# Where the first kernel of an S4 layer is loaded, and who adds the skip weights

## The chip, the cores and the metric

One core of a Trainium2 chip. The metric is the device time of one execution in microseconds, the median of several runs. A profile is one more execution, recorded instruction by instruction. Engines are named as in the profile: PE (matrix products; PEld its weight loads), DVE (vector), ACT (scalar functions), POOL (GpSimd) and SP (which here only issues DMAs).

## What is computed

Four layers in a row on x of 2048 positions by 640 channels, each with a layer norm and a residual: a long convolution with an S4 kernel, attention with one shared key and value head, the same convolution again, the same attention again.

```python
dt = jnp.exp(log_dt)[:, None]
P = jnp.exp((dt * A)[:, :, None] * l[None, None, :])
K = jnp.einsum("dn,dnl,dn->dl", Cc, P, dt * Bc).real     # kernel, 640 x 2048
...
y = irfft(rfft(pad(u)) * rfft(pad(K)))[..., :L] + u * Dskip
```

The convolution is done with Fourier transforms. Adding `u * Dskip` is the same as adding Dskip to the kernel's value at position 0, and this is how the program does it, before it transforms the kernels.

## The kernel before

The program has three parts that matter here.

The kernel generator, `_kgen`, makes K in 20 units on PE, ACT and DVE. Each finished unit is copied by ACT into a staging tile `kst`, and after units 7, 15 and 19 SP stores it into `kd` in device memory: five kernels of 128 channels each, 128 partitions by 16 positions by 128 channels. Position 0 is partition 0, the first 128 values. Kernels 0 and 1 are stored after the first 8 units, 2 and 3 after the next 8, kernel 4 at the very end, in four stores of short pieces (L436). During the generator POOL writes the constant first columns of the tables `c` and `s` (L362, L363), two memsets a unit. Near its end POOL issues the eight loads of the transform's weights `wf` (L527).

`kernel_spectra` loads the five kernels back, four into one tile `kts` and the fifth into `ktl`, adds the skip weights (`skip`, a one-row addition on DVE, L656), and transforms each: `raw` multiplies with `wf` on PE in four quarters (L545), ACT copies each quarter out of PSUM (L547), DVE does the butterflies `radix` (L555) and `fft8` (L96, L99) with two scratch tiles, `B` (16 KB a partition) and `R` (8 KB), and SP stores the spectrum into `kh`. The transform of kernel c + 1 on PE overlaps the butterflies of kernel c on DVE.

`conv_layer` then transforms x, multiplies, and transforms back, with the same `B` and `R`.

PE, ACT and DVE run in the order in which the code is written (`manual_schedule`). POOL and SP are queues of their own: a DMA that must wait for something holds everything behind it. The tiles of the convolution (`B`, `R`, `kts` under the tag "wi", `ktl` under "xn") lie in memory that the generator's tiles used before, so the first use of each waits until the generator's last use of that place is over. Such waits are found when the program is built: `B` lies on `kst`, `R` on the generator's rounding and fraction tiles, `kts` and `ktl` on its tables.

Of the kernel before, what the change touches and what calls it, by code (L numbers as in the profile page):

```python
# [11 lines left out]
F32 = mybir.dt.float32  # L12
# [4 lines left out]
ALU = mybir.AluOpType  # L17
# [4 lines left out]
P = 128  # L22
# [3 lines left out]
DC = 128  # L26
NCH = D // DC
# [57 lines left out]

def fft8(nc, A, B, R, sg):

    ADD, SUB = ALU.add, ALU.subtract
    plus, minus = (ADD, SUB) if sg < 0 else (SUB, ADD)
    calls = []

    def tt(*a):
        calls.append(lambda: nc.vector.tensor_tensor(*a))  # L96

    def stt(*a):
        calls.append(lambda: nc.vector.scalar_tensor_tensor(*a, op0=ALU.mult, op1=ADD))  # L99

    tt(B[:, 0:4], A[:, 0:4], A[:, 4:8], ADD)
    tt(B[:, 4:8], A[:, 0:4], A[:, 4:8], SUB)
    tt(R[:, 0:2], A[:, 10:15:4], A[:, 11:16:4], ADD)
    if sg < 0:
        tt(R[:, 2:4], A[:, 11:16:4], A[:, 10:15:4], SUB)
        tt(B[:, 12:16:3], R[:, 0:3:2], R[:, 3:0:-2], ADD)
        tt(B[:, 14:12:-1], R[:, 0:3:2], R[:, 3:0:-2], SUB)
    else:
        tt(R[:, 2:4], A[:, 10:15:4], A[:, 11:16:4], SUB)
        tt(B[:, 12:16:3], R[:, 2::-2], R[:, 1:4:2], SUB)  # L110
        tt(B[:, 14:12:-1], R[:, 2::-2], R[:, 1:4:2], ADD)
    tt(B[:, 8:12:3], A[:, 8:10], A[:, 13:11:-1], plus)
    tt(B[:, 10:8:-1], A[:, 8:10], A[:, 13:11:-1], minus)
    tt(A[:, 0:2], B[:, 0:2], B[:, 2:4], ADD)
    tt(A[:, 8:10], B[:, 0:2], B[:, 2:4], SUB)
    tt(A[:, 4:14:9], B[:, 4:6], B[:, 7:5:-1], plus)
    tt(A[:, 12:4:-7], B[:, 4:6], B[:, 7:5:-1], minus)
    sp, sm = (RT_HALF, -RT_HALF) if sg < 0 else (-RT_HALF, RT_HALF)
    f0, f2, f1, f3s = B[:, 8:10], B[:, 10:12], B[:, 12:14], B[:, 15:13:-1]
    stt(A[:, 2:4], f1, RT_HALF, f0)  # L120
    stt(A[:, 10:12], f1, -RT_HALF, f0)
    stt(A[:, 6:16:9], f3s, sp, f2)
    stt(A[:, 14:6:-7], f3s, sm, f2)
    return calls


def weave(calls, between):

    for i in range(len(calls) + 1):
        for n, call in between:  # L130
            if n == i or (i == len(calls) and n > i):
                call()
        if i < len(calls):
            calls[i]()


class Net:
# [153 lines left out]
    def _kgen(self, ctx):  # L291
        tc, nc, ins = self.tc, self.nc, self.ins
# [126 lines left out]
        def store(u):  # L419
            q, r, _, _, run = units[u]  # L420
            if r == 0 and q > 0:
                KST[q] = bp.tile([P, 32, run], F32, tag="kst", bufs=1, name=f"kst{q}")
            kst = KST[q]
            nc.scalar.activation(kst[:, :, 16 * r : 16 * r + 16],
                                 PK[u].rearrange("p (d j) -> p j d", d=16), AF.Copy)
            if 16 * (r + 1) == run:
                for par in range(2):
                    for jh in range(2):
                        src = kst[64 * par : 64 * par + 64, 16 * jh : 16 * jh + 16, :]
                        if run == 128:  # L430
                            dst = self.kd[2 * q + par, 64 * jh : 64 * jh + 64]
                            nc.sync.dma_start(dst, src.rearrange("p t d -> p (t d)"))
                        else:
                            dst = self.kd[4, 64 * jh : 64 * jh + 64].rearrange(
                                "p (t d) -> p t d", d=DC)[:, :, 64 * par : 64 * par + 64]
                            nc.sync.dma_start(dst, src)  # L436

# [3 lines left out]
        with tc.manual_schedule(engines=engines):  # L443
            for h in range(2):
                phase(0, h)
            for u in range(n + 3):
                now, nxt, prod, tot = u < n, u + 1 < n, 0 < u <= n, 2 <= u < n + 2
                odd = u % 2 == 1
                if u >= 3:
                    store(u - 3)  # L450
# [54 lines left out]
    def conv_setup(self, ctx):  # L505
        tc = self.tc
        if not self.wfs:
            self.conv_weights(self.nc.sync)
        self.cvp = ctx.enter_context(tc.tile_pool(name="cvp", bufs=1, reuse_waits="tile"))

        self.B = self.cvp.tile([P, 16, 256], F32, name="B")
        self.R = self.cvp.tile([P, 8, 256], F32, name="R")

    def conv_weights(self, eng, after=None):

# [121 lines left out]
    def load_spectrum(self, c):  # L637
        A = self.cvp.tile([P, 16, 256], F32, tag="kh", bufs=2, name=f"kh{c}")
        self.nc.sync.dma_start(A.rearrange("p s d -> p (s d)"), self.kh[c])
        return A  # L640

    def kernel_spectra(self):

        nc, cv = self.nc, self.cvp

        kts = cv.tile([P, 4, 16, DC], F32, tag="wi", name="kts")
        ktl = cv.tile([P, 24, DC], F32, tag="xn", name="ktl")
        ks = [kts[:, c] for c in range(4)] + [ktl[:, 0:16]]
        dsk = ktl[0:1, 16:21]
        nc.gpsimd.dma_start(dsk.rearrange("p c d -> p (c d)"), self.ins["A_Dskip"][None, :])  # L650
        for c in range(NCH):
            nc.gpsimd.dma_start(ks[c].rearrange("p t d -> p (t d)"), self.kd[c])

        def skip(c):
            k = ks[c][0:1, 0]
            nc.vector.tensor_tensor(k, k, dsk[:, c], ALU.add)  # L656

        skip(0)
        Z = {0: self.raw(ks[0], "k0")}
        for c in range(NCH):  # L660
            if c + 1 < NCH:
                skip(c + 1)
                Z[c + 1] = self.raw(ks[c + 1], f"k{c + 1}")
            A = cv.tile([P, 16, 256], F32, tag="kh", bufs=2, name=f"kn{c}")
            weave(self.radix(Z.pop(c), A) + fft8(nc, A, self.B, self.R, -1), ())
            nc.sync.dma_start(self.kh[c], A.rearrange("p s d -> p (s d)"))

    def conv_layer(self, nm, first):
# [1 line left out]


        tc, nc, cv = self.tc, self.nc, self.cvp
        B, R = self.B, self.R
        tt = nc.vector.tensor_tensor
        with tc.manual_schedule(engines={mybir.EngineType.PE, mybir.EngineType.Activation,
                                         mybir.EngineType.DVE}):
# [5 lines left out]
            self.norm_next(nm)  # L682
            if first:
                self.kernel_spectra()

            def X(c, tau):
                return self.x[:, tau, c * DC : (c + 1) * DC]
# [549 lines left out]
```

## Time and profile before

| | us |
|---|---|
| median of 3 runs | 3103.51 |
| lowest and highest run | 3099.85, 3104.56 |
| the profiled execution | 3100.43 |
| its span, first to last instruction | 3098.6 |
| PE busy in the span | 2850.6 (92%) |
| ACT busy | 2387.1 (77%) |
| DVE busy | 1436.4 (46%) |
| POOL busy | 41.8 (1%) |

Times in a timeline are counted from the start of the span. The generator runs until about 338, the kernels' spectra until about 437, the first convolution until 664; the first attention layer, the second convolution and the second attention layer follow. A row of the timeline gives start, length, engine, line, operation and tiles; in brackets stands how long the engine had been idle before and what it then waited for. Arrows read from the result: `zk<-kts,wf` is zk made from kts and wf.

### The profile page before, as it was taken

To read this page: it belongs to the slowest core of one execution; us is meant where nothing else is said; L and a number is where in the kernel's file an instruction comes from. 1 tells how busy PE (TensorE), PEld (TensorE's weight loads), DVE (VectorE), ACT (ScalarE), POOL (GpSimd) and SP (SyncE) were. 2 spreads that over 40 slices of the span, in tenths; PEclk is the share of its full clock that TensorE was granted. 3 is DMA by queue.
4 is the path that set the end of the run, shared out by engine and by line. 5 is a ranking of instruction groups with operands and counts; after the bars stand their busy time and mean duration, and the time that the engine had idled before them with its cause. 6 is when DMAs were issued, how large, how long until landed. Compare 5 with 4: busy or idle time off the path is not lost. (4 is left out here: it accounts for less than half of the span.)

```text
span 3098.6 us, 52133 instructions
## 1 busy us (share of the span) xinstructions
PE 2850.6 (92%) x21636; PEld 1349.7 (44%) x21636; DVE 1436.4 (46%) x1855; ACT 2387.1 (77%) x2769; POOL 41.8 (1%) x114
## 2 busy tenths in 40 slices
PE   2888998949899999999999899498999999999999
PEld 0555887847322333333333489464223333233333
DVE  7888799973122232232332399932222222222223
ACT  5777343224799999999999623055999999999997
POOL 0000000000100000000000000000000000000000
PEclk9999999979999999999999999799999999999999
DMA  6011451114310010100100210132010100100100
GB/s 142 18 29 24 168 218 55 33 30 131 116 27 25 21 26 23 25 25 21 27 25 22 111 55 28 26 111 89 22 27 23 40 25 21 44 25 21 44 18 22
DMA packets 73630, 153.45 MB, mean 50 GB/s; under 512 B 22836, under 2 KB 28980, under 8 KB 69764
## 3 DMA queue, kind: packets, MB, share of 16 engines
q1 hardware_dynamic: 67336, 132.36, 14.6%
q0 software_dynamic: 4080, 16.67, 1.4%
q8 instruction: 174, 2.85, 0.4%
q10 hardware_dynamic: 1968, 0.98, 0.1%
q14 instruction: 72, 0.59, 0.1%
HBM read 93.42 MB, written 44.50 MB: 45 GB/s over the span
## 5 line engine op out<-in xcount | busy, mean ns | idle before, releaser
L1038 ACT ACTIVATE pt<-scd 128x1024 f32<-128x1024 f32 x1024 | 942.2, 1116 | 7.5 <-PE scd L1034 5.8
L1038 ACT ACTIVATE pt<-scb 128x1024 f32<-128x1024 f32 x1024 | 942.2, 1116 | 7.0 <-PE scb L1034 5.4
L1048 PE MATMUL pod<-pt,vt 128*32 128x512 f32 x4096 | 547.1, 606 | 4.4 <-DVE on L1065 0.3
L1048 PE MATMUL pob<-pt,vt 128*32 128x512 f32 x4096 | 546.8, 606 | 4.4 <-DVE on L1065 0.5
L1034 PE MATMUL scd<-qpd,kt 62*128 62x512 f32 x2048 | 386.0, 451 | 6.0 <-PEq L983 5.6
L1034 PE MATMUL scb<-qpb,kt 62*128 62x512 f32 x2048 | 386.0, 451 | 5.8 <-PEq L983 5.5
L1034 PEld LDWEIGHTS scd<-qpd,kt 62*128 62x128 f32 x2048 | 166.0, 185 | 402.0 <-ACT pt L1038 392.6
L1034 PEld LDWEIGHTS scb<-qpb,kt 62*128 62x128 f32 x2048 | 166.0, 185 | 401.6 <-ACT pt L1038 392.4
L1096 DVE TENSOR_TENSOR x<-pyd,x 128x320 f32<-128x320 f32 x146 | 71.7, 491 | 561.1 <-PE pyd L1108 561.1
L1096 DVE TENSOR_TENSOR x<-pyb,x 128x320 f32<-128x320 f32 x146 | 71.7, 491 | 547.8 <-PE pyb L1108 547.8
L1068 DVE RECIPROCAL rc<-rc 128x512 f32<-128x512 f32 x62 | 207.9, 3353 | 2.1
L1048 PEld LDWEIGHTS pod<-pt,vt 128*32 128x32 f32 x4096 | 80.6, 108 | 178.2 <-issue 160.2
L1048 PEld LDWEIGHTS pob<-pt,vt 128*32 128x32 f32 x4096 | 80.6, 108 | 178.2 <-issue 160.2
L416 PE MATMUL pk<-s,m 128*64 128x32 f32 x1280 | 130.8, 295 | 13.3 <-DVE s L407 13.3
L416 PE MATMUL pk<-c,e1r 128*64 128x32 f32 x1280 | 132.1, 297 | 11.4 <-DVE c L406 11.2
L416 PEld LDWEIGHTS pk<-c,e1r 128*64 128x64 f32 x1280 | 105.3, 221 | 79.6 <-issue 52.1
L727 PE MATMUL ya<-Aa,wi 128*128 128x128 f32 x640 | 78.0, 285 | 50.5 <-DVE Aa L96 47.2
L727 PE MATMUL yc<-Ac,wi 128*128 128x128 f32 x640 | 78.4, 286 | 46.8 <-DVE Ac L96 43.7
L574 PE MATMUL za<-xna,wf 128*128 128x256 f32 x512 | 113.1, 383 | 2.3 <-ACT xna L690 2.3
L416 PEld LDWEIGHTS pk<-s,m 128*64 128x64 f32 x1280 | 108.1, 226 | 15.9 <-DVE s L407 15.9
L574 PE MATMUL zc<-xnc,wf 128*128 128x256 f32 x512 | 111.5, 379 | 2.7 <-ACT xnc L690 2.7
L576 ACT ACTIVATE Aa<-za 128x1024 f32<-128x1024 f32 x16 | 16.4, 1024 | 118.4 <-PE za L574 117.4
(276 smaller groups left out, 3170.6 us busy)
## 6 DMA issues: line engine op xcount, KB each, us to landing
kh<-kh SPq DMA_DIRECT2D x10, 2048.0 KB
kh<-kn SPq DMA_DIRECT2D x5, 2048.0 KB
qhd<-qh SPq DMA_DIRECT2D x40, 256.0 KB
qld<-ql SPq DMA_DIRECT2D x40, 256.0 KB
qpb<-qhd SPq DMA_DIRECT2D x256, 40.0 KB
qpd<-qhd SPq DMA_DIRECT2D x256, 40.0 KB
ot<-on SPq DMA_DIRECT2D x216, 40.0 KB
wf<-in_c_wf POOLq DMA_DIRECT2D x16, 512.0 KB, 7.8
```

The lines of the kernel that those rows point to most:

```text
L416: nc.tensor.matmul(PK[u][64 * par : 64 * par + 64, 32 * d : 32 * d + 32], e[u][:, d, par], c[u][:, d, par], start=first, stop=not first)
L574: nc.tensor.matmul(zv[:, :, c, kk], self.wf[:, t + 4 * h, j, c, kk], x, start=(n == 0), stop=(n == 3))
L576: nc.scalar.activation(A.rearrange("p (o s) d -> p o s d", o=2)[:, :, 2 * t : 2 * t + 2], z.rearrange("p (c o e) -> p o c e", c=2, o=2), A ...
L727: nc.tensor.matmul(y[:, s * DC : (s + 1) * DC], self.wi[:, t, j, c_, kk], v[:, 2 * t + c_, kk], start=(i == 0), stop=(i == 3))
L1034: nc.tensor.matmul(sc[:, 512 * par : 512 * par + 512], kt[rows, 128 * t : 128 * t + 128], qps[nb, hg, pr][rows], start=True, stop=True)
L1038: nc.scalar.activation(pt, sc, AF.Exp, scale=SCALE)
L1048: nc.tensor.matmul(po[32 * j : 32 * j + 32], vt[:, t], pts[step, j // 2][:, 512 * (j % 2) : 512 * (j % 2) + 512], start=(t == 0), stop=(t ...
L1068: nc.vector.reciprocal(rc, rc)
L1096: nc.vector.tensor_tensor(xh, py, xh, ALU.add)
```

## The change

Kernel 0 is no longer loaded into `kts` but into R's place: the scratch tile is now taken in two turns under one tag, first as the target of kernel 0's load, then, once PE has read it, as the butterflies' scratch. `kts` holds kernels 1 to 3, `ktl` kernel 4. The load of the skip weights into `ktl` and the five DVE additions are gone. Instead POOL issues five accumulating DMAs: for kernels 0 to 3 in the generator, right after their stores, onto the stored rows in `kd`; for kernel 4 after its load, onto the row in `ktl`. In the second convolution the scratch tile is taken in `conv_layer` rather than in `conv_setup`.

```diff
@@ store
+                for c in range(2 * q, min(2 * q + 2, NCH - 1)):
+                    self.skip(c, self.kd[c, 0:1, 0:DC])
@@ conv_setup
-        self.R = self.cvp.tile([P, 8, 256], F32, name="R")
+
+    def scratch(self, nm):
+        return self.cvp.tile([P, 8, 256], F32, tag="R", bufs=1, name=f"R{nm}")
@@ kernel_spectra
+    def skip(self, c, k):
+
+        self.nc.gpsimd.dma_start(k, self.ins["A_Dskip"][None, c * DC : (c + 1) * DC], accum_op=ALU.add)
+
+        ks = [self.scratch("k0").rearrange("p a b -> p (a b)").rearrange("p (t d) -> p t d", t=16)]
         kts = cv.tile([P, 4, 16, DC], F32, tag="wi", name="kts")
         ktl = cv.tile([P, 24, DC], F32, tag="xn", name="ktl")
-        ks = [kts[:, c] for c in range(4)] + [ktl[:, 0:16]]
-        dsk = ktl[0:1, 16:21]
-        nc.gpsimd.dma_start(dsk.rearrange("p c d -> p (c d)"), self.ins["A_Dskip"][None, :])
+        ks += [kts[:, c] for c in range(3)] + [ktl[:, 0:16]]
         for c in range(NCH):
             nc.gpsimd.dma_start(ks[c].rearrange("p t d -> p (t d)"), self.kd[c])
-
-        def skip(c):
-            k = ks[c][0:1, 0]
-            nc.vector.tensor_tensor(k, k, dsk[:, c], ALU.add)
-
-        skip(0)
+        self.skip(NCH - 1, ks[4][0:1, 0])
         Z = {0: self.raw(ks[0], "k0")}
         for c in range(NCH):
             if c + 1 < NCH:
-                skip(c + 1)
                 Z[c + 1] = self.raw(ks[c + 1], f"k{c + 1}")
             A = cv.tile([P, 16, 256], F32, tag="kh", bufs=2, name=f"kn{c}")
+            if c == 0:
+                self.R = self.scratch("k")
...
@@ conv_layer
             if first:
                 self.kernel_spectra()
+            else:
+                self.R = self.scratch(nm)
+            R = self.R
```

PE, ACT and DVE keep their order; what moves is POOL's queue and a few waits. First POOL, from the end of the generator to the kernels' loads, before. What an instruction waits for stands in brackets: an engine by its name, DMAs issued by SP as DMAHW with a lane's number, those issued by POOL as DMASW.

```order
L363 MEMSET s_19_2437 128x32 [waits DVE_49,Pool_49]
L527 DMA wf<-in_c_wf 128x1024 [waits DMAHW4_49,DMAHW3_49,DMAHW5_49,DMAHW2_49,DMAHW6_49,DMAHW1_49,DMAHW7_49,DMAHW0_49,PE_49]
L527 DMA wf<-in_c_wf 128x1024 x7
L650 DMA ktl<-in_A_Dskip 1x16x40 [waits DMASW0_49,DVE_49,PE_49]
L652 DMA kts<-kd 128x2048 [waits DMAHW6_49,DMAHW7_49,DMASW1_49,Pool_49]
L652 DMA kts<-kd 128x2048 [waits DMAHW1_49,DMAHW0_49,DMASW2_49]
L652 DMA kts<-kd 128x2048 [waits DMAHW3_49,DMAHW2_49,DMASW3_49]
L652 DMA kts<-kd 128x2048 [waits DMAHW5_49,DMAHW4_49,DMASW4_49]
L652 DMA ktl<-kd 128x2048 [waits DMAHW6_49,DMAHW1_49,DMAHW7_49,DMAHW0_49,DMASW5_49]
```

The same place in the changed kernel, where Rk is kernel 0's place in the scratch tile:

```order
L363 MEMSET s_19_2441 128x32 [waits DVE_49,Pool_49]
L648 DMA kd<-in_A_Dskip 16x8 [waits DMAHW4_49]
L531 DMA wf<-in_c_wf 128x1024 [waits DMAHW5_49,DMAHW3_49,DMAHW7_49,DMAHW1_49,PE_49]
L531 DMA wf<-in_c_wf 128x1024 x3
L531 DMA wf<-in_c_wf 128x1024 [waits DMASW0_49]
L531 DMA wf<-in_c_wf 128x1024 [waits DMASW1_49]
L531 DMA wf<-in_c_wf 128x1024 [waits DMASW2_49]
L531 DMA wf<-in_c_wf 128x1024 [waits DMASW3_49]
L659 DMA Rk_2718<-kd 128x2048 [waits DMASW4_49,DMAHW7_49,DVE_49,Activation_49]
L659 DMA kts<-kd 128x2048 [waits DMASW5_49,DVE_49,DMAHW1_49,Activation_49,Pool_49]
L659 DMA kts<-kd 128x2048 [waits DMAHW3_49,DMASW6_49]
L659 DMA kts<-kd 128x2048 [waits DMAHW5_49,DMASW7_49]
```

Before, every load of a kernel stood behind a DMA that waits for PE, the load of the skip weights into ktl. Now a wait for PE comes only with ktl's own load, the next row. The last four wf loads wait for the four accumulating transfers, whose lanes they use again (the third transfer stands one row ahead of the memset, the first two around the memset of unit 11).

Then DVE, from the end of kernel 0's `radix` into `fft8`, before:

```order
L555 TENSOR_TENSOR kn_2871<-Azk_2724 128x512 [waits Activation_49]
L555 TENSOR_TENSOR kn_2871<-Azk_2724 128x512
L96 TENSOR_TENSOR B<-kn_2871 128x1024 [waits DMAHW4_49,DMAHW3_49,DMAHW5_49,DMAHW2_49,DMAHW6_49,DMAHW1_49,DMAHW7_49,DMAHW0_49,DVE_49]
L96 TENSOR_TENSOR B<-kn_2871 128x1024
L96 TENSOR_TENSOR R<-kn_2871 128x512 [waits DVE_49]
```

And now:

```order
L559 TENSOR_TENSOR kn_2873<-Azk_2727 128x512 [waits Activation_49]
L559 TENSOR_TENSOR kn_2873<-Azk_2727 128x512
L96 TENSOR_TENSOR B<-kn_2873 128x1024 [waits DMAHW4_49,DMAHW3_49,DMAHW5_49,DMAHW2_49,DMAHW6_49,DMAHW1_49,DMAHW7_49,DMAHW0_49,DVE_49]
L96 TENSOR_TENSOR B<-kn_2873 128x1024
L96 TENSOR_TENSOR Rk<-kn_2873 128x512 [waits DMASW4_49,DVE_49,PE_49]
```

The first write of B waits for the stores of kernel 4 out of `kst` in both; the first write of R now also waits for kernel 0's load and for PE's last read of it. Elsewhere on DVE only the five additions are missing.

More of the change, by code (lines that the diff above doesn't have):

```diff
@@ L672, in conv_layer @@
         tc, nc, cv = self.tc, self.nc, self.cvp
-        B, R = self.B, self.R
+        B = self.B
         tt = nc.vector.tensor_tensor
```

## The prediction

> **What bounds the kernel now.** The page first, ACT's busy tenths in 40 slices:
>
> ```profile
> ACT  5777343224799999999999623055999999999997
> ```
>
> The nines are the two attention layers, most of the span, where ACT has hardly a pause. The change touches none of that; it touches the few microseconds where the kernel generator ends and the kernels' spectra begin, in the fifth slice. I cut that stretch out with the table by windows (columns: stretch, length, PE, PE weight load, DVE, ACT, POOL busy, granted clock, share of the DMA engines, GB/s).
>
> ```profile
> 338.59:344.68 6.09, 0.00 (x0) 0.00 (x0) 2.52 (x13) 2.09 (x3) 2.62 (x5) 1.00 0.66 226
> 351.60:374.40 22.80, 22.80 (x207) 22.80 (x205) 15.98 (x25) 6.15 (x6) 0.53 (x1) 1.00 0.33 92
> 374.40:437.40 63.00, 58.92 (x522) 58.26 (x520) 62.86 (x99) 24.53 (x37) 0.00 (x0) 1.00 0.61 234
> 437.40:664.50 227.10, 176.52 (x1040) 160.66 (x1041) 225.96 (x247) 56.23 (x116) 0.31 (x1) 0.89 0.16 55
> ```
>
> First PE stands still for 6.1 us; then PE is the busy engine until the first kernel is transformed; from 374 to 664 DVE never rests (62.86 of 63.00 us, 225.96 of 227.10). The list of waits says the same: DVE's only waits between 343 and 664 are these two, and PE's one wait for a load is the gap.
>
> ```profile
> DVE kn L555 <- ACT Azk L547: 10.8, 4, 4.0
> DVE kts L656 <- DMA kts<-kd: 4.8, 2, 2.5
> PE zk L545 <- DMA kts<-kd: 6.1, 1, 6.1
> ```
>
> So the end of this layer is set by one chain: load of kernel 0, PE's raw transform in four quarters, ACT's four copies, then DVE, which runs without a wait for some 300 us. Whatever brings the fourth copy forward brings all of DVE's work forward, and after 664 attention starts on what DVE left. The timeline shows that chain's head, and POOL's queue, which issues the loads:
>
> ```profile
> 302.74 0.16 POOL L362 MEMSET c<- 128x32 f32 x1 [6.79 <-DVE e1r L399]
> 309.92 0.16 POOL L363 MEMSET s<- 128x32 f32 x1 [7.02 <-DVE m L404]
> 319.53 4.37 POOL L527 DMA_DIRECT2D wf<-in_c_wf  x8 [9.45 <-PE pe L380]
> 338.24 0.30 PE L416 MATMUL pk<-s,m 128*64 128x32 f32 x2
> 338.63 0.51 POOL L650 DMA_DIRECT2D ktl<-in_A_Dskip  x1 [14.73 <-PE pk L416]
> 339.22 2.12 POOL L652 DMA_DIRECT2D kts<-kd  x4
> 344.68 0.58 PE L545 MATMUL zk<-kts,wf 128*128 128x128 f32 x1 [6.14 <-DMA kts<-kd]
> 350.54 1.02 ACT L547 ACTIVATE Azk<-zk 128x1024 f32<-128x1024 f32 x1 [9.83 <-PE zk L545]
> 354.05 1.02 ACT L547 ACTIVATE Azk<-zk 128x1024 f32<-128x1024 f32 x1 [2.49 <-PE zk L545]
> 357.63 1.02 ACT L547 ACTIVATE Azk<-zk 128x1024 f32<-128x1024 f32 x1 [2.55 <-PE zk L545]
> 361.20 1.02 ACT L547 ACTIVATE Azk<-zk 128x1024 f32<-128x1024 f32 x1 [2.55 <-PE zk L545]
> 363.47 2.35 DVE L96 TENSOR_TENSOR B<-kn 128x1024 f32<-128x1024 f32 x2
> 660.45 2.04 PE L727 MATMUL ya<-Aa,wi 128*128 128x128 f32 x8 [36.44 <-DVE Aa L96]
> ```
>
> The kernels' loads stand in POOL's queue behind the load of the skip weights into ktl, and that one waits 14.73 us for PE's last pk product. All four kts loads are held by a wait that only ktl's place in memory needs.
>
> **The change, part by part.** *The PE gap.* Kernel 0 now goes to R's place, and no load in front of it waits for PE: of the engines, its waits now name DVE and ACT alone. It can be issued right behind the wf loads (319.53 + 4.37 = 323.9) at the earliest, and at the latest when the generator's last products on DVE end:
>
> ```profile
> 330.44 1.21 DVE L407 TENSOR_TENSOR s<-s,m 128x1024 f32<-128x1024 f32 x1
> 330.00:332.00 2.00, 1.18 (x20) 0.94 (x19) 2.00 (x4) 0.60 (x1) 0.00 (x0) 1.00 0.93 361
> 332.00:334.00 2.00, 2.00 (x44) 2.00 (x41) 1.93 (x8) 0.00 (x0) 0.00 (x0) 1.00 0.06 23
> 342.00:344.00 2.00, 0.00 (x0) 0.00 (x0) 0.24 (x3) 0.00 (x0) 0.00 (x0) 1.00 1.00 411
> DMA to landing us min/median/max: 5.4/9.4/13.2
> ```
>
> That is 331.65. Both ends give the same landing, since the wf loads fill the DMA engines until 332. From there 1.05 MB at 411 GB/s take 2.55 us, so the data is across at 334.6; the shortest landing of a kts load, 5.4 us counted from 332, gives 337.4. Both lie ahead of 338.54, where PE's last pk product ends. The 6.14 us gap goes entirely. The wf loads were issued from POOL in 4.37 / 8 = 0.55 us each beside DVE's products, so I count no hold-up of POOL by DVE. [...]
>
> *The slow first quarter.* The first copy starts 5.86 us after PE's first matmul, the second 3.51 us later and the fourth 3.57 us after the third. In the group's row the slowest matmul takes just over twice the median:
>
> ```profile
> L545 PE MATMUL zk<-kts,wf x512: 275/275/582, 344.7 to 403.8; 128*128 128x128 f32 x171
> 347.00:348.00 1.00, 1.00 (x6) 1.00 (x6) 1.00 1.00 414
> 350.00:351.00 1.00, 1.00 (x11) 1.00 (x11) 1.00 1.05 431
> ```
>
> (The last two rows are slices of one microsecond for this line: PE, weight load, clock, DMA share, GB/s.) Six matmuls in one slice, eleven in the other, with the DMA engines equally full: so it is not the loads that slow PE, but the standstill before. Without a standstill the first quarter takes 3.57 us: 2.29 us less. The granted clock in these rows stays at 1.00 and does not show it. [...]
>
> *The skip additions on DVE.* Five one-row additions leave DVE. Two lie ahead of the chain, in DVE's wait. Three lie in the unbroken part:
>
> ```profile
> 374.29 0.27 DVE L656 TENSOR_TENSOR kts<-kts,ktl 1x128 f32<-1x128 f32 x1
> 374.49 0.67 DVE L555 TENSOR_TENSOR kn<-Azk 128x512 f32<-128x512 f32 x1
> 390.12 0.27 DVE L656 TENSOR_TENSOR kts<-kts,ktl 1x128 f32<-1x128 f32 x1
> 405.95 0.27 DVE L656 TENSOR_TENSOR ktl<-ktl 1x128 f32<-1x128 f32 x1
> ```
>
> Each shifts the next start by 0.20 us (374.29 to 374.49), three by 0.60. PE's pace of 4 x 3.57 = 14.3 us a kernel stays ahead of DVE's 15.6 (390.12 - 374.29 - 0.20), so DVE stays the bound.
>
> *The skip transfers on POOL.* Five accumulating transfers are added. The trace of before has no such transfer; the nearest row is the plain load of the skip weights, 1.7 us from issue to landing, and the farthest of the neighbourhood is 13.2 us. The third and fourth stand around the memset at 309.92 and wait for stores of the second pair of kernels:
>
> ```profile
> 312.00:315.00 3.00, 2.25 (x24) 1.15 (x22) 3.00 (x4) 1.70 (x3) 0.00 (x0) 1.00 0.00 0
> 328.17 1.22 DVE L404 TENSOR_TENSOR m<-m,s 128x1024 f32<-128x1024 f32 x1
> DMA to landing us min/median/max: 1.7/3.4/5.2
> ```
>
> (In the last row the first figure is the skip weights' load, the last one kernel 4's.) The stores' traffic is over by 312 (the first row has none); with a microsecond for the receipt, an estimate, the fourth transfer is issued by 313. Behind it on POOL stand the wf loads, which cannot go before 319.53 anyway: 6 us of cover. The memset behind the third is first read at 328.17: 18 us of cover. At 1.7 us the transfers have landed by 315, at 13.2 us by 326; that would hold the last wf load for some 3 us, while the ones before it keep the DMA engines full until past 330. I take 1.7, the nearest row, and a cost of nothing; the far end costs nothing either. The fifth runs in SBUF after ktl's load and is needed only by kernel 4, some 50 us later. A gain from them is excluded, as nothing waits for their results earlier than for the old additions.
>
> *A new neighbour for DVE's first B.* B lies where the last stores into kd read, and DVE's first write of B waits for those stores, before as after. Now it was due at 363.47 and found them done:
>
> ```profile
> 357.61 0.53 POOL L652 DMA_DIRECT2D ktl<-kd  x1 [16.27 <-DMA kd<-kst]
> 339.21 14.94 SPq L436 DMA_DIRECT2D kd<-kst  x4
> q1 hardware_dynamic: 1401, 0.35, 79.3%
> q1 hardware_dynamic: 992, 0.25, 71.8%
> ```
>
> With the gap gone it is due at 363.47 - 8.43 = 355.04. The stores were slow because the kts loads ran beside them; the last two rows are the SP queue (packets, MB, share) from 353 to 355, alone at 0.35 MB in 2 us, and from 355 to 357, where 0.25 MB were left: done at 356.4, landed 1.2 us later. In the new order the loads ahead end at 332 + 4.2 MB at 411 GB/s = 342.2, and the stores' 4 x 256 KB then take 6.0 us: done at 348.2, landed at 349.4. So 5.6 us of cover.
>
> **The sum.** 6.14 + 2.29 = 8.43 us for the fourth copy, 0.60 on DVE: 9.03 us. The profiled execution took 3100.43 us, of which 3098.6 are span: it would take 3091.4. The median of the runs shown is 3103.51, 3.1 above the profiled one; the same 9.0 off it gives 3094.5, which I forecast.
>
> **The rivals.** 0.2% of this kernel, about what a measurement can tell from no change, is 6.2 us.
>
> *The stores hold B.* If the last kd stores still land at 357.6, DVE gains only 363.47 - 357.61 = 5.86, plus 0.60: 6.5 us, 3097.0. For it: the wait is real. Against it: their competitor ends 10 us earlier. Chance 0.09.
>
> *The first quarter stays slow* though PE does not stand still: 6.14 + 0.60 = 6.7 us, 3096.8. Against it: slices with equally full DMA engines differ twofold. Chance 0.07.
>
> *The load does not come early*, because one of its waits is later than I read or it shares the engines with the other kernels' loads. If it lands at 341 to 344.6 the gain is 0.6 to 4.3 us: about 3101. Against it: both ends of the issue time give one landing. Chance 0.08.
>
> *Slower: an accumulating transfer that lands late.* The last wf load waits for the fourth one's landing T, and kernel 0's load stands behind it: it lands at about T + 0.55 (issue) + 1.3 (the wf load's 512 KB) + 5.4. PE starts later than at 338.54 from T = 331.3 on, and the kernel is slower from T = 338.1 on (344.68 + 0.60 - 7.25), 25 us after its issue; from there each microsecond costs one. At T = 350 it would be 12.0 us slower: 3115.5. Against it: the 1.7 and 13.2 us above. Chance 0.05.
>
> **How the numbers follow.** Forecast 0.71, the rivals 0.09, 0.07, 0.08 and 0.05. Low end: the lowest run shown, 3099.85, less 9.03 and less 1.2, a quarter of the runs' spread of 4.7, by which a median may lie lower: 3089.6. High end: the highest run, 3104.56, less the 6.5 of the first rival, is 3098.1; a part of the late loads takes it to 3099.5. Faster by over 0.2%: the forecast, and about half of the first two rivals, which lie right at 6.2: 0.79. Same: the other halves and the late loads, 0.16. Slower 0.05.
>
> **What would show it.** In the new profile PE's first zk matmul should start at 338.5 with no wait for a load, the first ACT copy at about 342.1 and the fourth at 352.8, DVE's first B at 355.0 without waiting for a DMA, and PE's first inverse matmul of the last chunk 9 us earlier than 660.45. A wait of zk for Rk, of B for kd stores, or wf loads issued after 319.5 names the rival that won. If all this holds and the time is still not 9 us shorter, something behind 664 took it back, and I was wrong there.

## The result, and the profile after

The median fell from 3101.91 us (17 runs, 3099.85 to 3105.51) to 3097.89 us (17 runs, 3092.51 to 3098.64). The ratio of the two kernels, which here and below is taken over all runs and not from the medians, is 0.9980, with an interval of 0.9973 to 0.9987, or 6.2 us (4.0 to 8.4). The medians alone show 4.0, because the runs of either kernel lie in two groups some 4 us apart and the two medians fall into different ones. The profiled execution took 3094.55 us (before 3100.43), its span 3092.8 (before 3098.6).

The head of the chain, in the timeline of the changed kernel (start, length, engine, line, operation, tiles; in brackets the idle time ahead and what ended it):

```profile
305.98 0.75 POOL L648 DMA_DIRECT2D kd<-in_A_Dskip  x1 [2.45 <-DMA kd<-kst]
311.00 0.76 POOL L648 DMA_DIRECT2D kd<-in_A_Dskip  x1 [0.29 <-DMA kd<-kst]
320.15 4.22 POOL L531 DMA_DIRECT2D wf<-in_c_wf  x8 [8.39 <-PE pe L380]
324.67 0.53 POOL L659 DMA_DIRECT2D Rk<-kd  x1 [0.29 <-issue]
330.64 1.57 POOL L659 DMA_DIRECT2D kts<-kd  x3 [5.44 <-DVE m L404]
339.11 16.15 PE L549 MATMUL zk<-Rk,wf 128*128 128x128 f32 x128
344.63 1.02 ACT L551 ACTIVATE Azk<-zk 128x1024 f32<-128x1024 f32 x1 [3.29 <-PE zk L549]
348.15 1.02 ACT L551 ACTIVATE Azk<-zk 128x1024 f32<-128x1024 f32 x1 [2.49 <-PE zk L549]
349.70 0.53 POOL L659 DMA_DIRECT2D ktl<-kd  x1 [17.49 <-DMA kd<-kst]
357.56 2.35 DVE L96 TENSOR_TENSOR B<-kn 128x1024 f32<-128x1024 f32 x2
373.20 2.35 DVE L96 TENSOR_TENSOR B<-kn 128x1024 f32<-128x1024 f32 x2
653.96 2.04 PE L733 MATMUL ya<-Aa,wi 128*128 128x128 f32 x8 [36.43 <-DVE Aa L96]
```

PE's first zk product follows the last pk product with no bracket: the gap of 6.14 us is gone. The profile puts 12.3 us between the issue of kernel 0's load at 324.67 and its landing, so it had landed at 337.0, where 337.4 was forecast and PE came at 339.1. But the first copy still comes 5.52 us after it (before 5.86), while the second follows 3.52 later. DVE's B has no bracket either: kernel 4's stores had landed by 349.70, when POOL passed its wait for them. The last chunk's first inverse comes at 653.96, 6.49 us earlier than before.

### The profile page after: what moved, and what is told of

Read it like the earlier page. It is cut to its first block, busy times and chain, and to the rows that moved or that the text cites. A ratio compares the mean times of both kernels' runs of the same rounds, so it can differ in the third digit from the quotient of the medians.

```text
span 3092.8 us, 52137 instructions
## 1 busy us (share of the span) xinstructions
PE 2850.0 (92%) x21636; PEld 1349.3 (44%) x21636; DVE 1435.6 (46%) x1850; ACT 2387.2 (77%) x2769; POOL 45.3 (1%) x118
## 5 line engine op out<-in xcount | busy, mean ns | idle before, releaser
L580 ACT ACTIVATE Aa<-za 128x1024 f32<-128x1024 f32 x16 | 16.4, 1023 | 118.6 <-PE za L578 117.4
```

Source lines behind the costliest of these rows:

```text
L580: nc.scalar.activation(A.rearrange("p (o s) d -> p o s d", o=2)[:, :, 2 * t : 2 * t + 2], z.rearrange("p (c o e) -> p o c e", c=2, o=2), A ...
```

## Experiments

Every gain below is against runs of the kernel before on the same chip; the runs were spread over several chips, so two versions are compared through their gains.

**Which half of the change does it.** One run keeps the accumulating transfers and loads kernel 0 into kts as before:

```diff
-        ks = [self.scratch("k0")...]
-        ks += [kts[:, c] for c in range(3)] + [ktl[:, 0:16]]
+        ks = [kts[:, c] for c in range(4)] + [ktl[:, 0:16]]
```

> The changed kernel, but kernel 0 is loaded into kts as before (kernels 0 to 3 in kts, kernel 4 in ktl); the accumulating transfers for the skip weights stay. Theory D (what freed the loads is that the load of the skip weights into ktl no longer stands ahead of them; R's place is not needed): the kts loads are issued about 330.6, when DVE's last use of their place ends, kernel 0 lands 5.4 us later at 336, ahead of PE's last pk product at 338.5; no gap, and the time of the changed kernel, 5.5 to 6.5 us under before, span about 3092. Rival E (R's place is needed, since the four kts loads share the engines and kernel 0 lands at the median of 9.4 us): kernel 0 at 340, a gap of 1.5 us, first B 1.5 us later, 4 to 5 us under before.

Its median was 3093.79 us; ratio to before 0.9975 (0.9966 to 0.9984), 7.8 us (5.0 to 10.5). From its timeline:

```profile
328.18 2.09 POOL L658 DMA_DIRECT2D kts<-kd  x4 [3.98 <-ACT c L372]
338.91 33.30 PE L549 MATMUL zk<-kts,wf 128*128 128x128 f32 x283
344.28 1.02 ACT L551 ACTIVATE Azk<-zk 128x1024 f32<-128x1024 f32 x1 [3.13 <-PE zk L549]
357.21 2.36 DVE L96 TENSOR_TENSOR B<-kn 128x1024 f32<-128x1024 f32 x2
```

The loads went out at 328.2, waiting for ACT and not for the DVE product that I had named, and kernel 0 was there when PE came. The other run keeps R's place, and puts the load of the skip weights and DVE's additions back:

```diff
+        nc.gpsimd.dma_start(dsk.rearrange("p c d -> p (c d)"), self.ins["A_Dskip"][None, :])
         for c in range(NCH):
             nc.gpsimd.dma_start(ks[c].rearrange("p t d -> p (t d)"), self.kd[c])
-        self.skip(NCH - 1, ks[4][0:1, 0])
```

> The other half of the change alone: kernel 0 goes to R's place, kernels 1 to 3 into kts, but the load of the skip weights into ktl stays ahead of all loads and DVE adds them as before; no accumulating transfers. Theory D (the wait of that load for PE is what holds the loads): PE's gap before kernel 0 stays at 6.1 us, first B and the time as before, gain 0. Rival E (R's place frees the load): the gap goes, gain 6 us.

Its median was 3100.57 us; ratio 0.9996 (0.9987 to 1.0005).

```profile
338.99 0.51 POOL L657 DMA_DIRECT2D ktl<-in_A_Dskip  x1 [14.73 <-PE pk L416]
339.52 0.55 POOL L659 DMA_DIRECT2D Rk<-kd  x1
344.96 16.18 PE L547 MATMUL zk<-Rk,wf 128*128 128x128 f32 x128 [6.06 <-DMA Rk<-kd]
```

The gap is back, though R's place had long been free (the changed kernel loads it at 324.67). So what closed the gap is that the load of the skip weights no longer stands in front, and the gain is that of the transfers; the new place for kernel 0 gave nothing by itself that these runs can tell (its interval goes from 4.0 us faster to 1.6 slower).

**Only moving that load.** The kernel before, with the skip weights loaded behind kernels 0 to 3:

```diff
-        nc.gpsimd.dma_start(dsk..., self.ins["A_Dskip"][None, :])
         for c in range(NCH):
+            if c == 4:
+                nc.gpsimd.dma_start(dsk..., self.ins["A_Dskip"][None, :])
             nc.gpsimd.dma_start(ks[c]..., self.kd[c])
```

> The kernel before with one line moved: the load of the skip weights into ktl is issued behind the loads of kernels 0 to 3 instead of ahead of them; DVE's additions stay, nothing is accumulated by DMA. Theory D: the kts loads go out at 330.6 as in the kernel without that load, PE's gap goes, and only the ninth product of kernel 0 (the first that reads position 0) must wait for the addition; the skip weights are issued at 338.6 and land 1.7 us later, so the addition is done at 341, and at half rate the ninth product is due at 342: no wait. Gain that of the changed kernel less the 0.6 us of the additions, about 5.5 us. Rival F (the small load lands behind the kernels' loads in the DMA queue, at 342 to 345): PE waits up to 3 us there, gain 3 to 5 us. Rival E as in the run beside it: kernel 0 lands at 340, gain about 4.

Its median was 3098.50 us; ratio 0.9989 (0.9980 to 0.9998), 3.4 us (0.6 to 6.2).

```profile
339.06 3.78 PE L545 MATMUL zk<-kts,wf 128*128 128x128 f32 x16
339.22 0.50 POOL L652 DMA_DIRECT2D ktl<-in_A_Dskip  x1 [6.54 <-PE pk L416]
345.17 0.48 DVE L657 TENSOR_TENSOR kts<-kts,ktl 1x128 f32<-1x128 f32 x2 [2.33 <-DMA ktl<-in_A_Dskip]
345.50 26.68 PE L545 MATMUL zk<-kts,wf 128*128 128x128 f32 x222 [2.66 <-DVE kts L657]
348.07 1.02 ACT L547 ACTIVATE Azk<-zk 128x1024 f32<-128x1024 f32 x1 [6.77 <-PE zk L545]
352.79 1.02 ACT L547 ACTIVATE Azk<-zk 128x1024 f32<-128x1024 f32 x1 [3.69 <-PE zk L545]
362.20 2.35 DVE L96 TENSOR_TENSOR B<-kn 128x1024 f32<-128x1024 f32 x2
```

Rival F won, and the 5.5 us of theory D did not come. PE starts at once, does eight products (recorded as 16), and waits 2.66 us for the addition, because the 2.5 KB of skip weights, issued while the kernels' loads were under way, became usable 5.95 us after their issue (339.22 to 345.17) instead of 1.7. The second copy then comes 4.72 us behind the first instead of 3.5, and the granted clock between 347 and 350 is 0.50: behind the wait PE lost its pace as well. Moving one line saved some half of the gain, with a wide interval; B comes 5.0 us later than with the transfers alone (362.20 to 357.21), because the addition is still on this path.

**Is PE at half rate when it leaves the generator?** The slow first quarter had not gone away with the standstill. I filled the gap of the kernel before with dense products:

```diff
+        warm = self.ps2("warm")
+        for n in range(14):
+            nc.tensor.matmul(warm[:, 0:P], self.wf[:, 0, 0, 0, 0], self.wf[:, 0, 0, 0, 1],
+                             start=True, stop=True)
         Z = {0: self.raw(ks[0], "k0")}
```

> The kernel before, with 14 dense 128x128 products of wf by itself put on PE between the last pk product and kernel 0's raw transform; their result is not used and nothing else changes. Theory A (PE comes out of the generator at half rate, whether or not it stands still, and some 3.8 us of dense products bring it to full rate): the first 8 or 9 of the 14 take 0.45 us each, the rest 0.22, 5.0 us in all, inside the 6.14 us gap; kernel 0's first ACT copy then starts 3.6 us after PE's first zk product (before: 5.86), DVE's first B and the end come 2.3 us earlier. Rival B (PE is at full rate after the generator and something of kernel 0's transform itself, the loads of the other kernels beside it, makes its first quarter slow): the 14 take 0.22 each, 3.1 us, and the first copy still comes 5.5 to 5.9 us after the first zk product; gain 0. Rival C (only the standstill slows it): all 14 at 0.22 from the first on, first copy after 3.6.

Its median was 3098.28 us; ratio 0.9989 (0.9980 to 0.9998), 3.4 us (0.6 to 6.2). From its timeline, and two slices of a microsecond for the line of zk (PE busy and the records that touch the slice, two for a product, weight loads, granted clock, DMA share, GB/s):

```profile
338.97 4.66 PE L661 MATMUL warm<-wf 128*128 128x128 f32 x28
345.09 19.14 PE L545 MATMUL zk<-kts,wf 128*128 128x128 f32 x169 [1.47 <-DMA kts<-kd]
349.03 1.02 ACT L547 ACTIVATE Azk<-zk 128x1024 f32<-128x1024 f32 x1 [7.82 <-PE zk L545]
345.00:346.00 1.00, 0.91 (x8) 0.91 (x9) 1.00 0.98 406
346.00:347.00 1.00, 1.00 (x12) 1.00 (x11) 1.00 1.00 414
```

The 14 products came right behind pk and still took 4.66 us; at 0.223 each (a full-rate quarter of 16 is 3.57) they would have taken 3.1, so some 7 ran at half rate. After them the slice from 346 has 12 records of kernel 0 where that of before from 347 had 6, with the DMA engines as full as ever, and its first copy comes 3.94 us after its first product: 1.92 sooner than before. Rivals B and C both fall. That 3.94, not 3.57, is what a first quarter costs at full rate.

The second test goes into the generator itself:

```diff
                 PK[u] = kp.tile([P, 512], F32, tag="pk", bufs=2, name=f"pk{u}")
+                for n in range({6: 16, 12: 16}.get(u, 0)):
+                    nc.tensor.matmul(PK[u][:, 0:P], self.ident, self.ident, start=True, stop=True)
```

> The kernel before, with 16 dense 128x128 products of the identity put on PE ahead of the pk products of units 6 and 12 of the generator; their result is overwritten. Theory A (the generator's small products leave PE at half rate): the first 8 or 9 of a burst take 0.45 us each, the rest 0.22. Then either A1, the pk products cannot hold the full rate: for a few microseconds 4 pk products take 0.21 instead of 0.43 us and a pair of 512-column products 0.6 instead of 1.03, then the old durations are back, and the whole is up to 5 us slower a burst; or A2, once at full rate they hold it: 0.21 for 4 pk products to the end of the generator, whose units are then set by DVE (12 of 14 us busy): 13 units some 1.5 us shorter, about 20 us faster. Rival C (the generator runs at full rate, as the recorded clock of 1.00 says): all 16 take 0.22 from the first on, and nothing after them is faster; 3.6 us slower a burst.

The one run took 3106.41 us, 3.3 over the median of before (3103.14): nothing of A2's 20 us. Selected rows of its timeline, around the first burst and behind the second:

```profile
156.42 1.03 PE L380 MATMUL pe<-kg,tm 48*128 48x512 bf16 x2
157.38 5.37 PE L414 MATMUL pk<-ident 128*128 128x128 f32 x32
162.94 0.29 PE L418 MATMUL pk<-c,e1r 128*64 128x32 f32 x4
163.06 0.29 PE L418 MATMUL pk<-s,m 128*64 128x32 f32 x4
163.51 0.60 PE L380 MATMUL pe<-kg,tm 48*128 48x512 bf16 x2
168.05 1.03 PE L352 MATMUL ph<-kg,ta 96*128 96x512 bf16 x2 [1.52 <-DVE f L357]
169.46 0.41 PE L418 MATMUL pk<-c,e1r 128*64 128x32 f32 x4
169.68 0.41 PE L418 MATMUL pk<-s,m 128*64 128x32 f32 x4
243.75 6.51 PE L414 MATMUL pk<-ident 128*128 128x128 f32 x32
255.55 0.60 PE L352 MATMUL ph<-kg,ta 96*128 96x512 bf16 x2 [1.52 <-DVE f L357]
257.44 1.03 PE L380 MATMUL pe<-kg,tm 96*128 96x512 bf16 x2
```

A pair of 512-column products takes 1.03 us ahead of the burst, 0.60 behind it, and 1.03 again at 168; the pk rows start 0.12 us apart behind the burst and 0.22 apart at 169.5. So the generator's products run at half rate, a dense burst lifts them, and the rate does not last: case A1. Two rows of the kernel before say that this holds from end to end and without standing still: none of 76 products of 512 columns took less than 604 ns (in the pair of 0.60 us they took 0.39 and 0.38 us), and from 320 to 330, in small products alone at the half pace, PE was busy for 10.00 of 10.00 us.

```profile
L380 PE MATMUL pe<-kg,tm x76: 604/620/634, 120.8 to 297.7; 48*128 48x512 bf16 x50, 96*128 96x512 bf16 x26
320.00:330.00 10.00, 10.00 (x194) 10.00 (x192) 6.59 (x7) 8.16 (x9) 3.90 (x8) 1.00 0.92 347
```

What takes the rate away again is not separated. Behind the first burst PE waits 1.52 us for DVE just before the slow pair; behind the second the pair after the same wait is still fast (255.55), and the pace halves soon after, while PE is busy. The small products or that wait could have done it.

The windows of the run with bursts show what misled me (granted clock in the third column from the end):

```profile
156.00:157.00 1.00, 1.00 (x12) 0.48 (x10) 1.00 (x1) 0.97 (x2) 0.00 (x0) 1.00 0.00 0
163.00:167.00 4.00, 3.52 (x80) 2.48 (x76) 1.46 (x2) 3.98 (x4) 0.04 (x1) 1.00 0.00 0
172.00:174.00 2.00, 1.96 (x22) 0.99 (x22) 2.00 (x3) 1.23 (x3) 0.00 (x0) 0.50 0.00 0
```

The same products at the same half pace are shown with clock 1.00 at 156 and 0.50 at 172. The trace's first record of the rate lies at 160.6 us here, and at 348.7 in the kernel before; ahead of it the column reads 1.00 without a record.

**A burst where it pays.** Added to the run with the transfers only, between the last two sets of pk products, where PE waits 0.8 us for DVE anyway (9 products; 13 in the other run):

```diff
+                for _ in range(9 if u == n - 1 else 0):
+                    nc.tensor.matmul(PK[u][:, 0:P], self.ident, self.ident, start=True, stop=True)
```

> The run with the transfers only (kernel 0 in kts), with 9 dense 128x128 products of the identity put on PE between the generator's next to last and last set of pk products, where PE waits 0.8 us for DVE anyway; their result is overwritten. Theory A: PE needs 7 to 13 such products at half rate (what the runs so far took, by where the burst fell) to reach full rate. If 9 are enough, they take 3.7 us, the last 64 pk products 3.8 instead of 6.9 us, so pk ends as before at about 338.5, PE stays at full rate into kernel 0, whose first copy starts 3.6 us after its first product instead of 5.4: everything after it 2 us earlier, about 3091.5. If 9 are too few, the last pk products stay at half rate and the burst is a loss: 4 us on PE less the 0.8 of waits, 3 us slower than the transfers alone. Rival C (the generator runs at full rate): the burst takes 2.0 us, pk its 6.9, about 1.2 us slower.

> The same with 13 dense products. Theory A: they bring PE to full rate wherever they fall, in 4.5 to 5.8 us; the last pk products then take 3.8 us and end 0.6 to 1.9 us later than without, and kernel 0's first quarter is 1.8 us shorter: between 1.2 us faster and no change against the transfers alone, 3092 to 3094. Rival C: 2.9 us for the burst, pk unchanged, about 2 us slower.

With 9 the median was 3091.16 us, ratio 0.9963 (0.9950 to 0.9977): 11.5 us (7.1 to 15.5), the lowest median of all. With 13 it was 3092.98, ratio 0.9974 (0.9964 to 0.9985), 8.1 us. Both intervals overlap that of the transfers alone (5.0 to 10.5), so the gain of a burst is read from the profile. The run with 9:

```profile
330.92 3.60 PE L414 MATMUL pk<-ident 128*128 128x128 f32 x18
338.30 33.88 PE L551 MATMUL zk<-kts,wf 128*128 128x128 f32 x301
342.24 1.02 ACT L553 ACTIVATE Azk<-zk 128x1024 f32<-128x1024 f32 x1 [1.59 <-PE zk L551]
355.16 2.35 DVE L96 TENSOR_TENSOR B<-kn 128x1024 f32<-128x1024 f32 x2
```

The burst takes 3.6 us, the pk products behind it give them back (zk starts at 338.30, without the burst at 338.91), kernel 0's first copy comes 3.94 us after its start, and B is 2.05 us earlier than with the transfers alone (357.21): the 2 us expected. The whole profiled execution was no shorter for it: its span is 3092.3 us, with the transfers alone 3092.0. At the head of the second attention layer the run with 9 does the same products at half pace that the other does at full; the first two rows are of the run with 9, the last two of the transfers alone.

```profile
2014.80 0.63 PE L912 MATMUL pqd<-xl,wh 128*52 128x512 f32 x1
2015.22 0.63 PE L912 MATMUL pqd<-xh,wh 128*52 128x512 f32 x1
2015.86 0.40 PE L910 MATMUL pqd<-xl,wh 128*52 128x512 f32 x1
2016.09 0.40 PE L910 MATMUL pqd<-xh,wh 128*52 128x512 f32 x1
```

The first of these products started 1.45 us earlier in the run with 9 (2013.90 against 2015.35), the sixteenth 1.29 us later (2020.14 against 2018.85). So an earlier start does not have to reach the end: PE's rate later on can differ too.

**The same at another place.** To that run, 150 dense products were added ahead of the last chunk's inverse in both convolutions:

```diff
+                if c == NCH - 1:
+                    warm = self.ps2(f"warm{nm}")
+                    for _ in range(150):
+                        nc.tensor.matmul(warm[:, 0:P], self.ident, self.ident, start=True, stop=True)
                 ys = [inverse(c, g, A) for g in range(2)]
```

> The run with the burst of 9, and in both convolutions 150 dense products of the identity on PE ahead of the last chunk's inverse, where PE stands still for 36 us waiting for DVE; their result is not used. At 0.22 us each they take 33 us and end 3 us before DVE's data comes. Theory A (a standstill or too thin work takes PE to half rate, dense products keep or restore full rate, and this holds anywhere in the kernel): the 64 products of the last inverse, 18.0 us from their first start to DVE's last residual addition at half and then full rate, take 14.7; some 3 us less in each convolution, 6 in all, about 3085. If DVE or the norms behind it set the pace there, or the rate at that place does not depend on what PE did before: no change, 3091; if the 150 take longer than 36 us, slower.

The median was 3091.89 us, ratio 0.9969 (0.9958 to 0.9981): no gain over the run with 9 that these runs can tell, and 7 us short of the 3085 expected. Its rows in the first and second convolution:

```profile
652.22 1.13 PE L734 MATMUL ya<-Aa,wi 128*128 128x128 f32 x8 [1.43 <-DVE Aa L96]
668.59 0.68 DVE L741 TENSOR_TENSOR x<-ya,x 128x512 f32<-128x512 f32 x1
1987.96 2.04 PE L734 MATMUL yc<-Ac,wi 128*128 128x128 f32 x8 [3.21 <-DVE Ac L96]
2005.80 0.69 DVE L741 TENSOR_TENSOR x<-yc,x 128x512 f32<-128x512 f32 x1
```

In the first convolution 1.43 us of standing still kept full rate: the first four products took 1.13 instead of 2.04, and from their start to the last residual it was 16.4 us. In the second, 3.21 us of standing still were enough to lose it: 2.04 again, and 17.8. So theory A holds in kind, but I had the gain at twice its size (1.6 instead of 3 us), and it was had at one place of two. Part of the missing 1.4 us is DVE: behind its first four products PE waited 1.19 us for it, in the run with 9 at the same place 0.36.

## Why the prediction was right, and where it was not

The forecast was 3094.5 with a range of 3089.6 to 3099.5. The time, 3097.89, lies in it, but the gain was 6.2 us and not 9.0, nearer to the 6.7 of the rival with the slow first quarter, whose time of 3096.8 the range held as well. That the number came out right is thus in part the width of the range. Whether the change belongs to "faster by over 0.2%", which had 0.79, or to "same" is open: 6.2 us is the line between the two. The steps:

- *The PE gap, 6.14 us*: went entirely, as worked out. The load into R's place was issued at 324.67, right behind the wf loads: the early end of the issue times worked out. The two halves taken apart show that what held the loads was the skip weights' load.
- *The skip additions on DVE, 0.60*: right. From one kernel's B to the next DVE now takes 15.64 us (357.56 to 373.20), 0.19 less than the 15.83 between the rows of before at 374.29 and 390.12.
- *The transfers on POOL, nothing*: right. The fourth was issued by 311.8, ahead of the 313 that counted an estimated microsecond from the end of the stores' traffic to their receipt (at kernel 4's stores before it was 1.2 us, 356.4 to 357.6), and the wf loads came when PE let them. Nor did DVE hold up POOL's loads: the three kts loads, issued from 330.64 beside two of DVE's TENSOR_TENSOR products, took 0.52 us each, and the load into R's place, issued while DVE waited, 0.53.
- *The cover of B, 5.6 us*: right in kind. The stores into kd had landed at 349.70, against 349.4 forecast, 7.9 us ahead of B.
- *The slow first quarter, 2.29*: this step failed. It became 0.34 (5.86 to 5.52). Even at full rate it could only have been 1.92, as a first quarter counted from PE's first product takes 3.94 us and not the 3.57 between two later copies. "So it is not the loads that slow PE, but the standstill before" ruled out the loads rightly and then took the only other cause that it had thought of. The run with bursts in the generator shows a third: PE comes out of the generator at half rate though it has been busy (its pk rows start 0.22 us apart, behind a burst 0.12), and the dense products of kernel 0 themselves have to raise it. The rival "the first quarter stays slow though PE does not stand still" is what happened; it had a chance of 0.07 and a time of 3096.8.

The sum so becomes 6.14 + 0.34 + 0.60 = 7.08. In the two profiles the first inverse of the last chunk shows 6.49, because the changed kernel's profile ran 0.62 us late from before the first transfer (the wf loads at 320.15 instead of 319.53). The run with 14 dense products, whose program is that of before up to 338, has 0.50 of this too (the skip weights' load at 339.13 instead of 338.63), so it belongs to the execution and not to the change. Behind that the lead shrinks to 5.8 us of span; I found no one place for it.

The trace of before could have hinted at the half rate ahead of the change. Its products of 512 columns start 0.40 us apart in the generator and 0.23 apart in the second attention layer, though with other operands and another type:

```profile
131.60 0.60 PE L380 MATMUL pe<-kg,tm 48*128 48x512 bf16 x1
132.00 0.63 PE L380 MATMUL pe<-kg,tm 48*128 48x512 bf16 x1
2022.43 0.39 PE L905 MATMUL pqd<-xh,wl 128*52 128x512 f32 x1
2022.66 0.39 PE L905 MATMUL pqd<-xl,wh 128*52 128x512 f32 x1
```

The experiments show both paces for one shape: the products pqd shown above start 0.42 and 0.23 us apart, and the two of a generator's pair 0.40 us apart in the pair of 1.03 us and 0.23 in that of 0.60. A product that is slow for its shape says more than a column that reads 1.00.

## What to carry to other kernels

A small load that must wait for a late engine holds every load behind it on its queue (here the queue stood for 14.73 us, and PE then for 6.14): take its result off the path, or put it behind them, which here kept some half of the gain, and look first at what stands ahead of the load that ends a wait. Do not count on PE's pace returning because it no longer stands still (here the first copy still came 5.52 us after PE's start, where full rate takes 3.94); look at how long a known product takes on both sides of the place, and if PE arrives at half rate, a few dense products (here 9, in 3.60 us) can pay for themselves where PE has enough work behind them before the next engine needs its result: here a wait of 0.8 us and the doubled pace of 64 products gave back 3.6 us. Split a change into halves: here one half brought a gain, and of the other none was seen.

## What the runs showed of the hardware

PE can be recorded as busy without a pause and run at half rate (10.00 of 10.00 us between 320 and 330). It took between 7 products (the bursts of 9 and 14, 3.60 and 4.66 us) and some 13 (the generator's second burst, 6.51 us for 16) to be lifted, by an estimate at 0.446 us each, twice the 0.223 of a product in a quarter of 3.57, 3.1 to 5.8 us. Behind 3.21 us of standing still in the second convolution the full rate was gone (2.04 us for the next four products); behind 2.66 us in the run with the skip load moved it was gone 1.5 us later (granted clock 0.50 from 347 to 350); behind 1.43 us in the first convolution it was still there (1.13 us for four), and so behind 1.47 us after the 14 products (12 records in the slice from 346). Why the counts and the pauses differ so was not shown. The 10 us of a PE busy with products of 32 columns did not raise the rate, where by that estimate 3.1 to 5.8 us of dense ones did. Which property of those products it is (32 columns, the shape 128*64 instead of 128*128, the weight loads between) was not tried.
